# Output projection of two thirds of the sequence rows moved into the spare rows of the recurrence's own output projection

## Chip, cores and metric

One NeuronCore of one Trainium2 chip (trn2). The metric is device time of one execution in microseconds (us); lower is better. The kernel runs 64 recurrent steps and everything around them, forward and backward, in one launch. "Stage" times below come from one traced execution of each kernel.

## The reference, cut to what matters

```python
# x (2048 x 640), mem0 (8 x 640), 32 heads of 128, segments of 32 rows
for s in range(64):
    h = concatenate([mem, xn[32*s:32*s+32]])           # 8 memory rows + 32 x rows
    q, k, v = h @ Wq, h @ Wk, h @ Wv                   # 640 -> 32 x 128
    p = softmax(mask(q @ k.T * scale)); o = p @ v
    o = o @ Wo                                         # 4096 -> 640
    mem = o[:8]                                        # carried to the next step
    outs.append(o[8:])
s = concatenate(outs)
out = x + s * silu(swiglu(xn))                         # g below
# the kernel returns out and the gradients of x, mem0, all weights
```

Only the 8 memory rows are recurrent. The x rows of a step can be computed at any time after its memory keys and values exist.

## The kernel before: the parts concerned

Rows are handled in 22 *tiles* of three segments (120 rows: 3 x 8 memory rows, 96 x rows), each tile cut into 8 *units* of four heads. In the forward loop a step's memory rows form a serial chain, and units of x attention are put as fill between its parts ("gaps" W0, W1, W2, G1 to G6). Three cuts:

```python
# --- one step t of the loop (cut) ---
def stage(): return ch.tile([P, 1024], BF16, name="stg", tag="stg", bufs=2)
sk = stage(); half(Wk_, 0, sk, 'v'); half(Wk_, 1, sk, 'v')
gap("W0")
sq = stage(); half(Wq, 0, sq, 'v')
...
dump(sk, k.KS[t])                     # k of the memory rows to memory, SyncE
half(Wq, 1, sq, 'v')
gap("W1")
sv = stage()                          # third tile of two buffers: waits for dump(sk)
...
k.copy(sv[:, 0:512], bA[:], eng='s')  # ScalarE
...
gap("W2")
#   memory scores -> psT
nc.scalar.copy(sTm[:], psT...)        # ScalarE
gap("G1")
#   softmax -> Pm; gap("G2"); transposes -> PTm; gap("G3")
for h in range(H):                    # memory PV: 32 matmuls, 8 columns each
    nc.tensor.matmul(pom[:, h, :], vt[:, h*P:(h+1)*P], PTm[:, h//16, :, h%16], ...)
oTm = ch.tile([P, H, 8], BF16, ...)   # 8 rows; the array's column group has 32
nc.vector.tensor_copy(oTm[:], pom[:])
packed_out(k, pm, oTm, Wo, True, True)   # O projection of the memory rows

# --- a unit of x attention: PV (L656 ff.) ---
for j in range(4):
    nc.tensor.matmul(po[:, j*P:(j+1)*P], PTs[qd%2][0:n, j, :], v[0:n, j*P:(j+1)*P], ...)
nc.scalar.copy(v[0:n], po[0:n])
nc.gpsimd.dma_start(k.OR[...], v[0:n])   # token-major rows, projected later

# --- the gaps of step t (cut) ---
if g == "W0":
    at(pv, t - 1, 0); at(turn_p, t - 1, 2)
    for u in kb[0:2]: ld_k(*u)           # SyncE: k rows of a later tile
elif g == "W1": at(pv, t - 1, 1)
elif g == "W2": at(pv, t - 1, 2)

# --- after the loop: output projection (cut) ---
for g in range(4): nc.sync.dma_start(k.QM[...], k.QVS[...])
nc.gpsimd.dma_start(WoT[:], ...)         # three weights at once, 15.7 MB
for nm_ in ("v", "k"): nc.gpsimd.dma_start(WT[nm_][:], ...)
blocks = [(3*b, 3, 96) for b in range(7)] + [(21, 1, 32)]
work = [(b, qd) for b in range(len(blocks)) for qd in range(8)]   # 64 units
# per unit: load rows of three tiles, 12 transposes, 3 copies, 20 matmuls
# per tile: epilogue out = x + s*g, gradient products, their transposes and stores
nc.gpsimd.dma_start(WT["q"][:], ...)     # fourth weight, then the next phase
```

## Time and profile before

| | before |
|---|---|
| median of the first three runs (range) | 6011.49 us (6007.91 to 6018.85) |
| start up to the first projection matmul of the loop | 614.9 us |
| forward loop, to the last v projection matmul | 1277.4 us |
| tail, to the first load of the output projection | 106.3 us |
| output projection, to the first matmul of the next phase | 264.7 us |
| that product (g0) and the preparation of the backward loop | 162.9 us |
| backward loop, then the rest | 1304.2 and 2276.6 us |

### The profile page before, as it was taken

What the parts mean: (1) busy time and instruction counts of PE and PEld (TensorE: products, weight loads), DVE (VectorE), ACT (ScalarE), POOL (GpSimd) and SP (SyncE); (2) the same over time, 40 slices, a digit from 0 to 9 for tenths busy, and PEclk for the clock granted to TensorE, in tenths of its full rate; (3) what the DMA queues carried; (4) which work ended last, traced back from release to release, by engine and by line L of the source; (5) the groups of instructions that cost most, each with busy time, mean ns of one, the idle gap of its engine ahead of it and who ended that gap; (6) DMA issues with size and microseconds to landing.
All of it is one profiled execution on the core that took longest, in us unless ns stands there. A gap on an engine that the chain in (4) does not pass through costs nothing. (4 is left out here: it accounts for less than half of the span.)

```text
span 6007.0 us, 166595 instructions
## 1 busy us (share of the span) xinstructions
PE 5182.7 (86%) x68354; PEld 3289.8 (55%) x68354; DVE 2394.8 (40%) x7496; ACT 1817.4 (30%) x4945; POOL 1038.9 (17%) x1654
## 2 busy tenths in 40 slices
PE   5969899999996775788888998799999999969899
PEld 2546455555553563555555665555566556637565
DVE  5723455555553333344444453322233223300351
ACT  2424355555553322222223332222232122200110
POOL 0000243434333201233333332000000000000000
PEclk9979899999998886888889998899999999989999
DMA  6565344444446453566556663532243323353332
GB/s 225 163 246 191 97 138 135 138 132 137 134 130 217 124 170 115 147 170 167 162 161 169 175 179 102 131 87 80 77 108 83 85 82 92 100 195 127 106 121 94
DMA packets 928035, 824.48 MB, mean 137 GB/s; under 512 B 403085, under 2 KB 819789, under 8 KB 923285
## 3 DMA queue, kind: packets, MB, share of 16 engines
q1 hardware_dynamic: 755904, 576.97, 32.8%
q0 software_dynamic: 53312, 118.39, 6.9%
q10 hardware_dynamic: 118057, 118.48, 6.2%
q8 instruction: 538, 8.81, 0.6%
q14 instruction: 224, 1.84, 0.1%
HBM read 509.44 MB, written 313.42 MB: 137 GB/s over the span
## 5 line engine op out<-in xcount | busy, mean ns | idle before, releaser
L1331 PE MATMUL wg<-gr,hr 120*128 120x512 bf16 (+1 forms) x2640 | 588.0, 383 | 16.6 <-DVE dST L1263 12.5
L1309 PE MATMUL g<-w,gT 128*128 128x320 bf16 x3840 | 555.6, 302 | 0.0
L1309 PEld LDWEIGHTS <-gT 128*128 128x128 bf16 x3840 | 372.2, 99 | 140.5
L1331 PEld LDWEIGHTS <-hr 120*128 120x128 bf16 (+1 forms) x2640 | 257.6, 99 | 338.9 <-issue 44.8
L1699 POOL TENSOR_TENSOR o<-gxn,ln_G 128x640 bf16<-128x640 f32 x16 | 22.4, 1398 | 2115.2 <-DVE gxn L1697 2115.2
L361 PEld LDWEIGHTS <-gkv 128*8 128x8 bf16 x8192 | 212.8, 98 | 154.6 <-DVE gkv L980 34.0
L90 DVE CAST wgo<-wg 128x512 bf16<-128x512 f32 x72 | 47.5, 688 | 582.8 <-PE wg L1331 295.0
L342 PEld LDWEIGHTS <-hx 128*32 128x32 bf16 x7680 | 178.0, 97 | 165.3 <-issue 5.2
L90 DVE CAST stg<-bank 128x512 bf16<-128x512 f32 x256 | 177.0, 692 | 201.9 <-PE bank L342 200.8
L1276 ACT CAST gr<-r6p 120x512 bf16<-120x512 f32 (+1 forms) x176 | 103.1, 586 | 490.8 <-PE r6p L1273 202.1
L361 PE MATMUL gbank<-WvT,gkv 128*8 128x320 bf16 x4096 | 227.8, 399 | 26.8 <-DVE gkv L980 26.8
L632 ACT ACTIVATE xP<-xsp,xnm 120x120 bf16<-120x120 f32 (+1 forms) x704 | 240.5, 376 | 10.4 <-DVE xnm L628 6.3
L1318 DVE TENSOR_TENSOR ghacc<-ghacc,g 128x320 f32<-128x320 f32 x240 | 117.0, 487 | 289.6 <-PE g L1309 289.6
L1419 PE MATMUL oa<-gow,orr 128*128 128x320 bf16 x1280 | 176.1, 301 | 54.3 <-DMA gow<-GWO 54.3
L92 ACT CAST wgo<-wg 128x512 bf16<-128x512 f32 x48 | 25.8, 589 | 634.9 <-PE wg L1331 634.9
L643 POOL TENSOR_TENSOR xP<-xP,xrz 120x480 bf16<-120x480 bf16 (+1 forms) x176 | 170.4, 968 | 158.9 <-ACT xP L632 107.8
L662 ACT CAST xv<-xpo 120x512 bf16<-120x512 f32 (+1 forms) x176 | 103.3, 588 | 298.8 <-PE xpo L660 247.8
L1115 DVE SCALAR_TENSOR_TENSOR gdS<-gdp,Dx,gPr 120x120 bf16<-120x120 f32 (+1 forms) x704 | 188.7, 330 | 0.0
L92 ACT COPY gT<-t6g 128x960 bf16<-128x960 bf16 (+5 forms) x216 | 167.3, 794 | 57.3 <-PE t6g L1292 55.3
L1419 PEld LDWEIGHTS <-orr 128*128 128x128 bf16 x1280 | 126.0, 98 | 104.5 <-issue 54.7
L1112 DVE CUSTOM_DVE_ANT_0 gdS<-gdp,gPr 120x120 bf16<-120x120 f32 (+1 forms) x704 | 153.5, 273 | 60.6 <-PE gdp L1101 59.9
L1087 POOL DMA_DIRECT2D VTD<-gvT x176 | 129.8, 739 | 272.5 <-ACT gvT L1086 247.1
(312 smaller groups left out, 10952.2 us busy)
## 6 DMA issues: line engine op xcount, KB each, us to landing
QVS<-stg SPq DMA_DIRECT2D x128, 256.0 KB
gqv<-QVS SPq DMA_DIRECT2D x112, 192.0 KB
vTt<-VTD SPq DMA_DIRECT2D x64, 320.0 KB
orr<-OR SPq DMA_DIRECT2D x16, 1280.0 KB
OR<-xv POOLq DMA_DIRECT2D x168, 120.0 KB, 2.9
VTD<-gvT POOLq DMA_DIRECT2D x168, 120.0 KB, 4.6
PR<-xP POOLq DMA_DIRECT2D x168, 112.5 KB, 5.0
gPr<-PR SPq DMA_DIRECT2D x168, 112.5 KB
```

Of the source, the lines that this page charges most:

```text
L90: return nc.vector.tensor_copy(out, in_)
L92: return nc.scalar.copy(out, in_)
L342: k.nc.tensor.matmul(bank[32 * g:32 * g + 32, :], x[:, dc, :], W[:, dc, c0:c0 + 512], start=(dc == 0), stop=(dc == k.DC - 1), tile_positio ...
L361: k.nc.tensor.matmul(pm[p0:p0 + nq, 0:320], x[:, h, :], W[:, h, 320 * b:320 * b + 320], start=(first and i == 0), stop=(last and i == 15), ...
L632: nc.scalar.activation(Pb[0:n, j, 0:n], sp[0:n, j, :], ACT.Exp, bias=nmx[0:n, j:j + 1], scale=k.scale, accum_out=Z[0:n, j:j + 1])
L643: nc.gpsimd.tensor_tensor(Pb[0:n, :, 0:n], Pb[0:n, :, 0:n], bc_last(rz[0:n], n), ALU.mult)
L1087: nc.gpsimd.dma_start(k.VTD[tl][:, :, h0:h0 + 4, :], vTq[:])
L1112: nc.vector.tensor_tensor_reduce(dS[0:n, j, :], dp[0:n, j, :], Pr[0:n, j, :], 1.0, 0.0, ALU.mult, ALU.add, Dx[0:n, j:j + 1])
L1115: nc.vector.scalar_tensor_tensor(dS[0:n, j, :], dp[0:n, j, :], Dx[0:n, j:j + 1], Pr[0:n, j, :], op0=ALU.subtract, op1=ALU.mult)
L1309: nc.tensor.matmul(pg[:], ring[:, i, j, r0:r0 + P], Ws[qd][i][:, j, 320 * h:320 * h + 320], start=(i == 0 and j == 0), stop=(i == 2 and j ...
L1331: nc.tensor.matmul(accs[dc][:], hr[0:n, tl, dc * P:(dc + 1) * P], st["g", NTL * qd + tl, i][0:n, :], start=(tl == 0), stop=(tl == NTL - 1))
L1419: nc.tensor.matmul(ac[j][i][:], orr[:, w, jj * P:(jj + 1) * P], gow[:, w, 320 * i:320 * i + 320], start=(w == 0), stop=(w == NW - 1))
```

## The change

The memory rows' O projection uses 8 of the 32 rows (weight columns) of each column group, and the time of its matmuls hangs on the 320 columns streamed, hardly on those (the 64 matmuls of a step span 2.35 us at the median). So 24 x rows of an older step are to ride along for nothing. For tiles 0 to 13 the PV of a unit is also made transposed, stored, and read back as 24 columns of the weights; their projected rows leave the loop finished, and the output projection after it has 32 units instead of 64. To make room, `vt` is folded over two row groups (half the bytes per partition), so the memory PV runs on two row groups. The output projection is rewritten: one epilogue a unit, in a fixed order, inputs loaded one tile ahead, its stores issued by SyncE, weight fetches cut into 13 pieces.

```diff
-        vt = st.tile([40, HD], BF16, name="vt")
+        vt = st.tile([104, HD // 2], BF16, name="vt")
+        oTm = st.tile([P, H, 32], BF16, name="oTm")
@@ memory PV
-            PTm = ch.tile([40, 2, 8, 16], BF16, name="PTm", tag="PTm")
-            nc.scalar.copy(PTm[:].rearrange("p a q h -> p a (q h)"), ps3[:])
+            PTm = ch.tile([104, 8, 16], BF16, name="PTm", tag="PTm")
+            for a in range(2):
+                nc.scalar.copy(PTm[64 * a:64 * a + 40].rearrange("p q h -> p (q h)"), ps3[64 * a:64 * a + 40])
-            for h in range(H):
-                nc.tensor.matmul(pom[:, h, :], vt[:, h * P:(h + 1) * P], PTm[:, h // 16, :, h % 16], start=True, stop=True)
-            nc.vector.tensor_copy(oTm[:], pom[:])
+            for j in range(16):
+                for a in range(2):
+                    p0 = 64 * a
+                    nc.tensor.matmul(poms[a][:, j, :], vt[p0:p0 + 40, j * P:(j + 1) * P], PTm[p0:p0 + 40, :, j],
+                                     start=True, stop=True, tile_position=(p0, 0))
+            nc.vector.tensor_copy(oTm[:, 0:16, 0:8], poms[0])
+            nc.vector.tensor_copy(oTm[:, 16:32, 0:8], poms[1])
@@ the ride
+        def oride_ld(t):
+                nc.sync.dma_start(r[:], k.OTX[t - k.OT0])               # in gap W0
+        def oride(t):
+                nc.gpsimd.tensor_copy(oTm[:, :, 8:32], uu.pop(("o", t))[:])   # in gap G1
@@ pv
+            if 4 * tl < k.NO:
+                for j in range(4):
+                    nc.tensor.matmul(pt[:, j, :], v[0:n, j * P:(j + 1) * P], PTs[qd % 2][0:n, j, 24:120], start=True, stop=True)
+                nc.scalar.copy(ot[:].rearrange("p c h t -> p h c t"), pt[:].rearrange("p h (c t) -> p h c t", t=24))
+                nc.scalar.dma_start(k.OTX[4 * tl:4 * tl + 4, :, 4 * qd:4 * qd + 4, :]..., ot[:]...)
@@ output projection (cut)
-        blocks = [(3 * b, 3, 96) for b in range(7)] + [(21, 1, 32)]
+        blocks = [(tl, 3, 96) for tl in range(NRT, k.NTL - 3, 3)] + [(k.NTL - 2, 1, 96), (k.NTL - 1, 1, 32)]
+            if tl < NRT:
+                s_tok = io.tile([96, D], BF16, name="s_tok", tag="s_tok", bufs=2)
+                for b in range(2):
+                    nc.scalar.dma_start(s_tok[:, 320 * b:320 * b + 320], k.FS[t0:t0 + 4, 32 * b + 8:32 * b + 32, :])
+            for _ in range(2):
+                if i >= 2 and fetch:
+                    nc.gpsimd.dma_start(*fetch.pop(0))
+            for (f, o) in ((ep_ld, -1), (ep_b, 0), (ep_c, 1), (ep_d, 2)):
+                if i - o in slot:
+                    f(slot[i - o])
```

## The prediction

> **What bounds the kernel now.** I read the page first: one core, span 6007.0 us, TensorE 86% busy. An average over stages says little, so I took the table of windows to cut the span, then inside the stages that the diff touches the groups of instructions, the waits and the timeline, engine by engine. The columns of the table are the window, its length, then busy us (and count) of TensorE, weight loads, VectorE, ScalarE and GpSimd, the granted clock, the DMA share and GB/s.
>
> ```profile
> 1000.00:1300.00 300.00, 284.51 (x5187) 165.23 (x5183) 170.66 (x503) 157.52 (x545) 124.23 (x179) 0.99 0.45 134
> ...
> 1900.00:1960.00 60.00, 9.69 (x77) 6.52 (x77) 4.81 (x16) 9.41 (x39) 13.96 (x16) 0.50 0.88 317
> 1960.00:1999.00 39.00, 18.83 (x222) 13.18 (x222) 9.98 (x42) 21.85 (x102) 20.34 (x33) 0.50 0.29 67
> 1999.00:2030.00 31.00, 24.46 (x228) 19.06 (x229) 5.73 (x16) 3.83 (x8) 0.55 (x1) 0.83 0.42 119
> ...
> 2060.00:2230.00 170.00, 143.36 (x1609) 117.17 (x1608) 66.45 (x172) 42.48 (x87) 14.88 (x17) 0.97 0.51 154
> 2230.00:2263.00 33.00, 4.54 (x88) 3.60 (x87) 4.64 (x13) 2.96 (x7) 4.33 (x4) 0.50 0.63 206
> ```
>
> Four pieces matter. The **forward loop** runs from 614.5 us (first projection matmul) to about 1900: 64 steps of some 20 us, TensorE 95% busy. The **tail**, the last tile's softmax and PV after the last step, goes to 1999; its first 60 us are DMA at 317 GB/s with TensorE idle: the 15.7 MB of transposed weights for the next phase (three of 128x5x4096 elements of 2 bytes) are fetched at once there, and the tail's small loads stand behind them:
>
> ```profile
> 1908.74 16.03 SPq L591 DMA_DIRECT2D xv<-QVS  x1
> ```
>
> The **output projection** goes from the first load of attention rows at 1998.6 to the first matmul of the next phase at 2263.3, 265 us, for 64 work units; its last 22 us are again idle behind a weight fetch:
>
> ```profile
> 1998.57 1.34 SPq L772 DMA_DIRECT2D orow<-OR  x3
> ...
> 2263.29 5.28 PE L891 MATMUL g0pb<-WoT,g0x 128*128 128x512 bf16 x12 [22.04 <-DMA g0x<-GST]
> ```
>
> What comes after (backward loop, weight gradients) the diff leaves alone. In the loop, the memory rows of a step make a serial chain (projections, scores, softmax, PV, output projection, next step), with x-row work as filler. TensorE waits there little; the fillers on ScalarE are nearly as long as the chain. From the groups of 1000 to 1600 us (30 steps; busy, mean ns, then idle before and its releaser):
>
> ```profile
> L660 PE MATMUL xpo<-xv,xPT 120*128 120x128 bf16 x316 | 31.4, 222 | 0.0
> L662 ACT CAST xv<-xpo 120x512 bf16<-120x512 f32 x79 | 46.5, 589 | 132.3 <-PE xpo L660 96.2 <-DMA OR<-xv 23.7 <-DMA KS<-stg 9.7
> L585 ACT COPY kT<-kpt 128x384 bf16<-128x384 bf16 x79 | 34.7, 478 | 4.1 <-PE kpt L583 4.1
> L545 ACT COPY PTm<-bank 40x256 bf16<-40x256 bf16 x30 | 11.0, 366 | 6.8 <-PE bank L543 6.8
> L551 DVE CAST oTm<-bank 128x256 bf16<-128x256 f32 x30 | 12.7, 424 | 11.5 <-PE bank L549 11.5
> ```
>
> **What the Trainium skill says.** (1) "TensorE: Matmul & The Clock Gate", Part 1, "Wait — 56ns, not 53.3ns?": starts of matmuls never come closer than about 25 ns, however small. The trace agrees: the 32 memory-PV matmuls of 8 columns take 1.00 us, less a latency of 0.17 over 31 gaps, 27 ns each. So placing them on two row groups of the array, as the change does, wins nothing. (2) "TensorEngine Tiling (Array Packing)", Key Properties: changing the tiling mode drains the array; the change adds two such changes a step. No row before prices one. (3) "DMA: Bandwidth & Descriptors", "Queues, rings and completion order": each DMA engine takes turns between queue rows at packet granularity. The trace agrees with sharing and no priority: the small load above took 16.03 us to issue beside the weight fetch. (4) "SBUF — State Buffer", the summary of rules: GpSimd and a two-port VectorE copy exclude each other. The new GpSimd copy of 128x768 lands near the eight small VectorE copies of the v rows (291 ns each); what that costs, the trace before cannot say.
>
> **Part by part: the loop.** For tiles 0 to 13 of 22 (steps 4 to 45, 42 steps) each of the 112 PV units gets four more matmuls of 96 columns. Four of 128 columns span 0.40 us less 0.22 of latency, so about 60 ns apart; four of 96 cost about 0.17 us of TensorE. ScalarE gets a copy of 384 columns (0.48 us, the kT row) and the issue of a store (0.44 us, the ACT issue of a load in the later stage). Three units come in two steps of three, two in the third.
>
> In a step of three units the third sits just before the memory scores' copy sTm, in ScalarE's written order. In the timeline, PV ends at 1244.44 us, two stg copies fill ScalarE until 1245.2, then xv, then
>
> ```profile
> 1245.57 0.37 ACT L520 CAST sTm<-bank 40x256 bf16<-40x256 f32 x1
> ```
>
> After the change TensorE comes 0.3 to 0.5 us later (2 to 3 times 0.17), and 0.9 us of new ScalarE work stands ahead of sTm, so sTm comes about 1.3 us later. Not all of it reaches the end: VectorE is busy with v copies until about 1247.05 anyway, and TensorE idles 0.68 us before the transposes of Pm. I carry 0.65 us. In a step of two units no PV stands there: 0.35 us. Then in every step: PTm in two copies of 128 columns instead of one of 256 (from the 256 and 512 rows, 366 and 589 ns, about 0.26 each; the pair of stg copies shows 0.11 us of overlap, so 0.04 more), oTm in two copies (424 against 691 ns for 512 columns gives 0.29 each, so 0.16 more). Sum: 0.85 and 0.55, mean 0.75 us. For drains, the locked port, later loads (each OTX store is 512 pieces of 192 bytes; SyncE issues twice as many v loads) I add 0.25: 1.0 us times 42 = 42 us. The other 22 steps carry 0.2 plus 0.15: 8 us. The output projection of the step keeps its cost: 64 matmuls of 320 columns, four at a time, 16 times 133 ns = 2.1 us against 2.35 seen; 32 columns of weights for 8 change only weight loads that lie under it. **Loop: +50 us.**
>
> **The tail.** The weights come in 13 pieces issued between the tail's own GpSimd instructions, not in three lumps. The instruction order shows, though, that the first piece still goes before the last step's probabilities are stored. The bytes are the same: 15.7 MB at 317 GB/s are 50 us, and the tail from 1901 to 1999 has some 50 to 60 us of work of its own (1949 to 1999 is undisturbed, and does most of it). They overlap better, yet not fully. **Tail: -12 us**, a choice between 0 and -40.
>
> **The output projection.** Work units fall from 64 to 32: two blocks of three tiles (16 units), 8 units of one tile, 8 of 32 rows. A full unit took (2230 - 1999)/57, about 4.0 us, with TensorE at 20 matmuls of 120 ns plus 12 transposes, about 3.0. If the epilogue were free, 40 units of 4 us would be saved, 160 us. It is not: 22 epilogues that were three per eight units come now one per unit. Each costs ScalarE six load issues (0.44 each, 2.6 us) and copies of 0.56 and 0.48, about 3.7 us; VectorE four of 0.49 and two oT copies, 2.7 us; and 0.49 MB of inputs, 0.12 of s rows and 0.37 of stores beside 0.29 of attention rows, 1.27 MB, which at 300 GB/s is 4.2 us. So ScalarE, DMA and TensorE all stand near 4; in one order with few buffers I take 4.6 us for the 16 full units (74), 4.2 for the four after (17), 1 for the other 12 (12), 9 for start and cold clock (0.55 in the first 30 us before), and 24 for the end behind the last weight fetch, which is unchanged (22 before). Sum 136 against 265: **-129 us**.
>
> **Sum.** 6011 - 129 - 12 + 50 = 5920 us, 1.5% less.
>
> **Rivals.** (A) *The loop gives it back.* If ScalarE's store issues also wait for earlier DMAs[...], sTm's whole 1.3 us and more arrive on the chain: 2 us times 42 plus 10 is +94, total about 5965. For it: ScalarE already waits on the KS store (15.5 us in those 30 steps) and its softmax ends at 1253.63, just when the output projection does (1253.46). Against: ScalarE is only 52% busy. (B) *The epilogue becomes the bound.* Loads waiting for the previous tile's loads at 6 us a tile give 20 times 6 in place of 91: 5950. For it: before, ScalarE's gzT copy stood 3.96 us behind load and store issues. (C) *All hidden*: the tail loses its 40 us of stall, extra matmuls slip under waits (0.5 us a step): 5865. Against: TensorE has 5% idle in the loop.
>
> **Range and chances.** The terms err by about 30 (loop), 20 (projection), 15 (tail); in quadrature near 40, so 8 in 10 is about 55 us to either side: 5865 to 5975. Faster by over 2% means below 5891, 29 us under my number: 0.24. Slower by 2% needs a loop cost of over 300 us: 0.02. Within 2%: 0.74.
>
> **What would show it.** In the changed profile: loop period up by about 1 us between steps 8 and 45 and by 0.3 after; a wait of the transposes of sTm on ScalarE that was nearly absent; memory PV still 27 ns a matmul; the projection stage about 136 us, ScalarE issuing loads most of the time; the tail 90 to 100 us. I am wrong if the loop's period rises by over 2 us (A), a tile's epilogue takes over 6 us (B), or the tail falls to 70 us (C).

## More of the kernel before

The stages are cut at instructions that every version has: the first and last matmul that makes the loop's bank from a weight and the step's rows, the first load of attention rows, the first matmul of g0, and so on. A change in one stage can then be read from that stage, while the 86% of TensorE over the whole span tells nothing on it. Two lines of the loop's waits are needed below, from the table of waits over 600 to 1960 us (engine, line, what it waited for: us in total, times, longest):

```profile
ACT stg L92 <- DMA KS<-stg: 28.2, 15, 3.3
PE bank L526 <- ACT sTm L520: 4.0, 7, 1.1
```

In the first line ScalarE's copy of v into its stage tile waits until the dump of k has landed, since three stage tiles share two buffers. 28 us in a loop of 1277 look harmless. In the second, TensorE waits for ScalarE's copy of the memory scores.

## The result, and the profile after

| | before, same chip | after |
|---|---|---|
| median (range) of 4 runs, all fast | 6015.09 us (6007.91 to 6018.85) | 5968.41 us (5955.75 to 5980.50) |
| ratio, 95% interval | | 0.9924 [0.9899, 0.9948] |

The kernel is 0.8% faster. Ratios here are the mean of one kernel's fast runs over the mean of the other's in the same rounds, so not quite the ratio of the medians. The prediction, 5920 us, was 48 us too low; its range held.

| stage, us (one trace each) | before | after | measured change | predicted |
|---|---|---|---|---|
| forward loop | 1277.4 | 1335.5 | +58.1 | +50 |
| tail | 106.3 | 110.5 | +4.2 | -12 |
| output projection | 264.7 | 150.6 | -114.1 | -129 |
| sum of the three | | | -51.8 | -91 |
| start | 614.9 | 619.3 | +4.4 | none |
| everything after | 3743.7 | 3762.6 | +18.9 | none |

The traces differ by 28.5 us, the medians by 46.7: the traced run of before (6008.71 us, taken beside the four) was near the fastest, that of after the slowest. The 18.9 us lie in code that the change leaves alone. Other traces of kernels that share this code have 2276.6 to 2299.7 us in the last part alone, and the kernel before with nothing but two loads of its loop moved (below) has 3763.1 us in everything after. So I take the 18.9 us for the spread of single traces, the 4.4 us of the start too (613.7 to 622.2 in the runs below without initialising stores), and explain only the three stages. They have a spread as well: the same loop took 1335.5 and 1330.3 us in two traces, the same output projection 149.9 to 157.6 in seven.

First the windows of the changed kernel (columns as in the prediction): a piece of the loop, the tail in two pieces, most of the full units of the output projection, the last full and the short ones, and its end.

```profile
1000.00:1300.00 300.00, 269.44 (x4993) 165.94 (x5019) 165.27 (x489) 165.60 (x566) 121.00 (x167) 0.98 0.53 150
...
1955.00:2000.00 45.00, 15.51 (x196) 10.51 (x193) 11.02 (x37) 15.65 (x63) 19.81 (x26) 0.60 0.79 258
2000.00:2030.00 30.00, 7.81 (x90) 5.44 (x91) 4.47 (x16) 9.19 (x47) 10.22 (x15) 0.50 0.65 203
...
2066.00:2140.00 74.00, 48.78 (x487) 38.52 (x488) 32.73 (x79) 12.57 (x27) 0.00 (x0) 0.90 0.84 231
2140.00:2193.00 53.00, 34.17 (x559) 30.43 (x555) 24.60 (x65) 12.80 (x25) 0.31 (x1) 0.81 0.60 164
2193.00:2216.00 23.00, 0.42 (x7) 0.42 (x8) 1.84 (x4) 0.97 (x2) 1.43 (x1) 0.57 0.77 256
```

The stretch of full units has TensorE busy 66% (48.78 of 74) where before it was 84%, and the DMA engines 84% where before they were at 51%. The tail's small loads still stand behind the weight fetch (timeline of SyncE), and at the end TensorE is still idle for 18.6 us in one piece beside a fetch (timeline of TensorE):

```profile
1965.10 10.19 SPq L611 DMA_DIRECT2D xq<-QVS  x1
```

```profile
2215.91 4.47 PE L965 MATMUL g0pb<-WoT,g0x 128*128 128x512 bf16 x10 [18.61 <-DMA gqv<-QVS]
```

In the loop, groups of 1000 to 1600 us (28 steps), answering to those of the prediction:

```profile
L693 ACT CAST xoT<-xot 128x384 bf16<-128x384 f32 x72 | 34.6, 481 | 95.3 <-PE xot L691 94.9 <-DMA OTX<-xoT 0.4
...
L691 PE MATMUL xot<-xPT,xv 120*128 120x96 bf16 x288 | 24.8, 209 | 0.0
L682 POOL COPY oTm<-oride 128x768 bf16<-128x768 bf16 x28 | 23.3, 831 | 0.0
...
L562 ACT COPY PTm<-bank 40x128 bf16<-40x128 bf16 x56 | 14.5, 259 | 8.3 <-PE bank L559 8.0
...
L570 DVE CAST oTm<-bank 128x128 bf16<-128x128 f32 x28 | 8.2, 292 | 8.6 <-PE bank L568 5.5 <-ACT xP L652 0.2
...
L542 PE MATMUL bank<-ident,sTm 40*128 40x40 bf16 x58 | 6.3, 184 | 15.6 <-ACT sTm L536 15.6
```

The durations are those predicted (0.48 us for the added ScalarE copy, 0.26 and 0.29 for the halved copies), and the predicted wait for sTm is there: 15.6 us in 28 steps, which the same group of the kernel before had at 1.6 in 30. What the prediction did not have is the growth of another line, in the same table of waits as above:

```profile
ACT stg L92 <- DMA KS<-stg: 37.4, 21, 5.7
...
PE bank L542 <- ACT sTm L536: 23.9, 36, 2.6
```

And memory PV on two row groups (timeline of TensorE, one step of before, one of after; start, us):

```profile
1106.15 1.00 PE L549 MATMUL bank<-PTm,vt 40*128 40x8 bf16 x32
```

```profile
1108.24 0.67 PE L568 MATMUL bank<-PTm,vt 40*128 40x8 bf16 x32 [0.30 <-ACT PTm L562]
```

The same 32 matmuls take a third less, where the prediction saw nothing to win.

### The profile page after: what moved, and what is told of

It reads as the page before. It is cut to its first block, busy times and chain, and to the rows that moved or that the text cites. A ratio compares the mean times of both kernels' runs of the same rounds, so it can differ in the third digit from the quotient of the medians.

```text
span 5978.5 us, 165521 instructions
## 1 busy us (share of the span) xinstructions
PE 5060.8 (85%) x67367; PEld 3238.0 (54%) x67644; DVE 2395.6 (40%) x7482; ACT 1840.4 (31%) x5059; POOL 1045.7 (17%) x1647
## 5 line engine op out<-in xcount | busy, mean ns | idle before, releaser
L1405 PEld LDWEIGHTS <-hr 120*128 120x128 bf16 (+1 forms) x2640 | 258.7, 99 | 343.2 <-issue 51.8
L663 POOL TENSOR_TENSOR xP<-xP,xrz 120x480 bf16<-120x480 bf16 (+1 forms) x176 | 170.0, 966 | 162.8 <-ACT xP L652 95.6
L529 DVE COPY vt<-stg 8x512 bf16<-8x512 bf16 x512 | 162.8, 318 | 51.4 <-ACT stg L92 44.0
```

Of the source, the lines that this page charges most:

```text
L529: nc.vector.tensor_copy(vt[p0:p0 + 8, c0:c0 + 512], sv[32 * g:32 * g + 8, b * 512:(b + 1) * 512])
L663: nc.gpsimd.tensor_tensor(Pb[0:n, :, 0:n], Pb[0:n, :, 0:n], bc_last(rz[0:n], n), ALU.mult)
L1405: nc.tensor.matmul(accs[dc][:], hr[0:n, tl, dc * P:(dc + 1) * P], st["g", NTL * qd + tl, i][0:n, :], start=(tl == 0), stop=(tl == NTL - 1))
```

## The experiments

Each run is timed beside the kernel before on its chip: four executions of each experiment, and seven of the kernel before for the batch. Ratios are to the kernel before; the changed kernel has 0.9924.

### First batch: take parts of the change away

**The added PV away, zeros ride** (the rows that ride are zeros). Its output is wrong, which doesn't matter for the time.

```diff
+        for i in range(k.NO):                      # before the loop
+            nc.gpsimd.dma_start(k.OTX[i]..., kTs[0]...)
-            if 4 * tl < k.NO:                      # xot matmuls, copy, store: gone
-                ...
```

> The changed kernel without the extra PV work (no 96-column matmuls, no ScalarE copy, no store to OTX; OTX is filled once with zeros, so the result is wrong on purpose). The step's output projection still carries 32 rows, the GpSimd copy and its load stay. Loop = first Wk matmul to last Wv matmul: 1277.4 us before, 1335.5 after. Theory (the extra PV units are the loop's cost, 0.9 us in each of 42 steps, as the shortest periods of the two traces say): loop about 1295, the last 20 us being later transfers and the wider step. Rival (the ride itself, its GpSimd copy, load and 32 rows, is the cost): loop over 1320.

Measured: 5996.55 us (5986.24 to 6011.45), ratio 0.9956; the start is 23 us longer by the 56 initialising stores, so only the loop counts. It fell by 11 us only, to 1324.6. A tile goes by in three steps, so there are three kinds of step: the first and the second with three PV units, the third with two. Periods (from one step's write of the next step's rows to the next) of the early steps did fall by what the PV should cost (steps 4 to 20, lower quartiles of the three kinds: 20.95, 20.29, 20.24 to 20.15, 19.33, 19.59), but in steps 21 to 45 those of the first kind grew (21.29 to 22.83). The time came back in one wait:

```profile
ACT stg L92 <- DMA KS<-stg: 56.2, 25, 5.6
```

This points to a step that is not the sum of its engines' work: in some steps with most fill, the landing of the dump of k would be a second bound (tested in the second batch). The sequence shows in the changed kernel's SyncE timeline of one such step:

```profile
1332.58 0.34 SPq L677 DMA_DIRECT2D oride<-OTX  x1
1332.97 1.34 SPq L275 DMA_DIRECT2D kr<-KS  x2
1335.40 0.34 SPq L501 DMA_DIRECT2D KS<-stg  x1
```

and in ScalarE's, the copy that needs the dumped buffer:

```profile
1340.97 1.07 ACT L92 CAST stg<-bank 128x512 bf16<-128x512 f32 x2 [1.03 <-DMA KS<-stg]
```

The loads for the ride and for k stand ahead of the dump in one queue, and the copy waits 5.6 us after the dump's issue.

**No ride at all, but the split, the fixed order and the paced fetch kept.**

```diff
-        self.OTX = mk("OTX", (self.NO, P, H, 24))
+        self.NO = 0
-        blocks = [(tl, 3, 96) for tl in range(NRT, k.NTL - 3, 3)] + ...
+        blocks = [(3 * b, 3, 96) for b in range(7)] + [(21, 1, 32)]
```

> Nothing rides: all 22 tiles go through the output projection, 64 units as before, but with the new order of the epilogue, the fetches in pieces, the memory PV on two row groups and the 32-row step. Theory: loop 1277 to 1290; projection about 250 (before 264.7), since an epilogue of a tile costs more than the 4.0 us unit it stands beside; tail about 108 as in both; in all within 20 us of before. Rival (the fixed order is what won the 114 us of the projection): projection under 200 and time under 5950.

Measured: correct, 6039.98 us (6034.39 to 6045.05), ratio 1.0029. Output projection 255.9 us: all of its rewriting but the halved units is worth 9 us, so these carry 105 of the 114. Steps without this wait were shorter than before in the second kind (19.42 against 19.57 us, means of steps 21 to 45), yet the loop was 7 us longer (1284.8), again with a longer wait for the dump (40.4 us from step 21 on, 26.1 before). That left the price of the split open until the last batch.

**The memory PV unsplit, a badly made test.** To fit, both halves of v were put in the same partitions, one over the other.

```diff
-        vt = st.tile([104, HD // 2], BF16, name="vt")
+        vt = st.tile([40, HD // 2], BF16, name="vt")
-                    dst = vt[64 * i + 8 + a:64 * i + 8 + b, :]
+                    dst = vt[8 + a:8 + b, :]
```

> The changed kernel with the memory PV back on one row group: one transposed PTm of 256 columns in one copy, 32 matmuls in a row, one VectorE copy of oTm. For want of room the v rows of heads 16 to 31 lie over those of heads 0 to 15, wrong on purpose; loads and copies are as many. The prediction (the split wins nothing and costs 0.2 us a step): loop 13 us shorter than 1335.5. The trace of the changed kernel (32 matmuls in 0.67 us, not 1.00, and steps that carry no extra PV 0.16 us shorter than before): loop 5 to 12 us longer.

Measured: 6169.59 us (6167.17 to 6184.79), ratio 1.0247, loop 1517.1 us. Its time tells nothing of row groups: the second load of a step had to wait for the first, and SyncE stood still (its waits):

```profile
SPq L473 <- DMA vt<-QVS: 270.0, 86, 5.5
```

The values were wrong by this as well, though within the tolerance of the comparison. The loop's 182 us more come with this stall; as the run also let PTm share a buffer with sTm, they are not split up. One thing it does show: with the changed kernel around them, the 32 matmuls on one row group take 1.00 us again (median of 64 steps; 0.67 on two), so the 0.33 us are the split's.

**The written order kept from the loop through the output projection**, so that the fetch cannot slip into the tail.

```diff
-        start = len(nc.cur_bb.bb.instructions)
+        start = k.start3 = len(nc.cur_bb.bb.instructions)
-        in_order(k, start)            # of the output projection
+        in_order(k, k.start3)
```

> The changed kernel, but each engine has to keep the written order from the loop to the end of the output projection, so that no weight fetch is issued before the tail's own GpSimd work is through. Theory (the tail is long because its small loads share the DMA engines with the fetches): tail from 110.5 to about 65 us; the same bytes then fall on the projection, which grows from 150.6 to 180 or 200; in all 10 us faster to 10 us slower. Rival (the tail is a chain of its own and the fetch lies beside it): tail over 95.

Measured: correct, 5995.60 us (5981.90 to 6014.96), ratio 0.9955. The tail fell from 110.5 to 62.0 us, the output projection rose from 150.6 to 209.8: together 271.8 against 261.1. The windows of both stages:

```profile
1955.00:2017.00 62.00, 40.43 (x543) 26.15 (x544) 24.24 (x84) 35.52 (x150) 31.16 (x46) 0.66 0.37 99
2017.00:2227.00 210.00, 94.90 (x1062) 75.31 (x1062) 60.46 (x154) 29.61 (x72) 25.99 (x39) 0.70 0.80 241
```

The tail has 62 us of work of its own and moves 5.1 MB for it. In the changed kernel it takes 48.5 us more and moves 24.9 MB: besides the 15.7 MB of weights, a copy of 4.2 MB (QM) falls there, as in the kernel before. 19.8 MB in 48.5 us are 408 GB/s. At 317 GB/s, the mean of the kernel before over 60 us, they would take 63 us; at 431, its fullest slice of 2.7 us, 46 (both estimates). So little of the fetch is hidden behind the tail's own work, at most some 14 us.

### Second batch: one wait at a time

**The third unit's PV after the memory scores.**

```diff
-                at(pv, t - 1, 2)      # gap W2
                 ride_ld(t + 1)
             elif g == "G1":
                 oride(t)
+                at(pv, t - 1, 2)
```

> Only the place of the third unit's PV (with its added xot matmuls) in a step changes: after the copy of the memory scores instead of ahead of it. Theory L1 (a step is as long as the sum of its engines' work on the path, as predicted): the wait for the ScalarE copy of the memory scores (18.5 us in 21 steps after the change, 2.6 us before) goes, the loop falls from 1335.5 by 10 to 18 us, the time by as much. Theory L2 (in the three-unit steps the landing of the dump of k is a second bound): that wait goes too, but the wait of ScalarE's stage copy for the dump grows from 31.6 us by most of the gain, and the loop falls by at most 6 us.

Measured: correct, 5973.68 us (5969.59 to 5982.30), ratio 0.9916. The loop stayed (1339.6). In the window 1045 to 1930 us the wait for sTm fell from 18.5 to 5.3 us, and the wait for the dump did not grow but fell (31.6 to 24.7). So neither theory had the mechanism; other steps lengthened (second kind, steps 21 to 45, mean 20.50 to 21.75), and I did not find by what.

**The loads one gap later, behind the dump of k.**

```diff
             if g == "W0":
-                oride_ld(t)
                 at(pv, t - 1, 0)
                 at(turn_p, t - 1, 2)
-                for u in kb[0:2]:
-                    ld_k(*u)
             elif g == "W1":
+                oride_ld(t)
+                for u in kb[0:2]:
+                    ld_k(*u)
                 at(pv, t - 1, 1)
```

> The loads of the ridden tile and of two k tiles are issued one gap later, so that the dump of k goes to its queue ahead of them; nothing else changes. L2: the wait of the stage copy for that dump (31.6 us in 20 steps) falls under 10 us, and the loop falls by 15 to 25 us to 1310 to 1320, the time by as much. L1 or 'the dump is late for another reason' (bandwidth, not order): the wait stays over 22 us and the loop stays within 6 us of 1335.

Measured: correct, 5947.02 us (5940.32 to 5953.61), ratio 0.9870 [0.9853, 0.9887]. The loop fell by 27.1 us to 1308.4, more than the 15 to 25 expected. SyncE's timeline has the dump first:

```profile
1325.24 0.34 SPq L501 DMA_DIRECT2D KS<-stg  x1
1325.69 0.37 SPq L677 DMA_DIRECT2D oride<-OTX  x1
1326.10 1.68 SPq L275 DMA_DIRECT2D kr<-KS  x2
```

and in the table of waits over 600 to 1960 us the wait is all but gone:

```profile
ACT stg L92 <- DMA KS<-stg: 2.1, 4, 1.3
```

Shown, then, as the bytes stayed: the place of the loads ahead of the dump made the wait, and it cost the changed kernel about 27 us of loop in these traces (by the two timed ratios 0.5%, some 30 us).

**Epilogue inputs two tiles ahead, three buffers.**

```diff
-                t_ = io.tile([96, D], BF16, name=f"ep_{nm_}", tag=f"ep_{nm_}", bufs=2)
+                t_ = io.tile([96, D], BF16, name=f"ep_{nm_}", tag=f"ep_{nm_}", bufs=3)
-            for (f, o) in ((ep_ld, -1), (ep_b, 0), (ep_c, 1), (ep_d, 2)):
+            for (f, o) in ((ep_ld, -2), (ep_b, 0), (ep_c, 1), (ep_d, 2)):
```

> The epilogue's loads in the output projection are issued two tiles ahead instead of one, with a third buffer. Theory P1 (latency: VectorE stands for the tile of results that the loop left in memory, and the copies of the next unit stand behind it in its written order): a full unit falls from 5.2 to 4.4 us, the stage from 150.6 to about 138, the time by 10 to 14. Theory P2 (bandwidth: a full unit moves 0.30 MB of rows and about 1.05 MB for one epilogue tile, at the 231 GB/s of that stretch 5.8 us): the stage stays within 4 us of 150 and VectorE only waits elsewhere.

Measured: correct, 5973.92 us (5958.98 to 5979.99), ratio 0.9918: no difference from the changed kernel's. The sixteen full units fell from 85.1 to 79.2 us, the stage only by 3.1 to 147.5. Other traces agree: 85.1, 86.7 and 89.4 us where the loads come one tile ahead, 79.2 and 81.8 where two. But most of it only moved: the start of the stage, to the first matmul of a unit, grew from 6.4 to 11.0 us (10.6 in the trace with 81.8). Latency is a small part of a unit, 0.4 us of 5.3 at most, and net of the start about 0.1.

**The fetch later and in paces** (strict order; 5.2 MB over the loop's drain, the rest beside the second half of the output projection and beside g0).

```diff
+            if t - T < DC:                         # drain of the loop
+                nc.gpsimd.dma_start(k.WoT[:, t - T], src[:, t - T])
+            if i >= 16 and i % 2 == 0 and fetch and i < 31:
+                nc.gpsimd.tensor_copy(dm[:], st["t", ...][0:1, 0, 0:8])   # paces the next line
+                nc.gpsimd.dma_start(*fetch.pop(0))
```

> The written order holds from the loop through the output projection, and the weights for the backward loop are fetched later and in paces: one of them over the drain of the loop, one and the query copy in the second half of the output projection, two beside the product that follows. Theory F1 (the tail's 110 us and the 22 us ahead of the next product are fetched bytes that compete with the path): tail 60 to 70, output projection 125 to 150, next product and its sequel (162 us together) up to 15 longer; time 55 to 85 below the changed kernel, 5885 to 5915. Theory F2 (the same bytes only move on, as they did with the strict order alone): tail 62, but the sum of tail, projection, product and sequel stays within 20 us of the changed kernel's 423.

Measured: correct, 5977.56 us (5952.03 to 5990.75), ratio 0.9916. Tail 80.8, output projection 166.9, g0 and preparation 169.0: 416.7 against the changed kernel's 423.0 from the end of the loop to the backward loop. F2 holds in the sum: the bytes move on (its tail of 62 did not come, as the first weight lay there). The tail is again nearly a plain sum: 62 for itself and 18.8 for 5.2 MB (16.5 at 317 GB/s).

### Third batch: with the dump ahead of the loads

**The same reordering in the kernel before** (the edit above without `oride_ld`).

> The kernel before, with the k loads one gap later and nothing of the change. The kernel before lost 26.1 us in 13 steps to the wait for the dump of k, so L2 expects its loop to fall from 1277 to 1250 to 1260 and the time by 15 to 25 us. With the loop of the changed kernel so ordered (1308.4) that leaves 50 to 58 us for the change in the loop, as predicted (50). If instead the loop stays at 1270 or more, the wait was made large by the change and the ride costs under 40 us without it.

Measured: correct, 6005.14 us (6002.23 to 6015.99), ratio 0.9969. The loop fell by 13.9 us to 1263.5; the expected 17 to 27 was too much, since of 23.6 us of wait that went, about 10 had not shown in the loop:

```profile
ACT stg L92 <- DMA KS<-stg: 4.6, 4, 1.5
```

So with this wait out of both kernels the change costs the loop 1308.4 - 1263.5 = 44.9 us. Of the 58.1 measured, the other 13.2 are the second bound, which bit harder once the ride put more in front of it. A difference of four single traces with some 5 us of spread each would be weak alone, but the timed runs say the same: with the loads moved in both kernels their ratios stand at 0.9870 to 0.9969, which is 0.9901 where it was 0.9924, 14 us.

**No added PV, loads moved** (wrong).

> Wrong on purpose: the changed kernel without the added PV (rows of zeros ride instead), now with the k loads one gap later. Without the late dump taking the time back, L2 expects the removal to shorten the loop by 0.65 to 0.97 us in each of 42 steps, 27 to 41 us below 1308.4, to 1267 to 1281; with the loads as they were it had taken off only 11. If the loop falls by under 15 us, something else than the dump gave the time back.

Measured: 5940.24 us (5939.24 to 5942.08), ratio 0.9863. The loop fell from 1308.4 to 1276.5 us, by 31.9: the removal that had brought 11 us now brings its price, 0.76 us in each of 42 steps. L2 is confirmed by this run and by the move of the loads (its sizes for the later PV and for the kernel before missed).

**Both moves**, and **both moves with early epilogue loads**.

> The changed kernel with both moves: k loads one gap later, third unit's PV after the memory scores. The dump's wait being gone, the removal of the wait for the score copy (5.8 us in 16 steps are left of it with the k loads moved) should now show in full: loop 1300 to 1305, time 3 to 8 us below the k loads alone. If the loop is 1308 or more, the copy's wait is hidden anyway and the place of that PV is worth nothing.

> Both moves and the epilogue's loads two tiles ahead: the candidate for a version that beats both kernels. Loop as in the run with both moves, output projection 3 us shorter; time 5940 plus or minus 10, ratio to the kernel before 0.984 to 0.988.

Measured, both correct: 5946.75 us (5934.71 to 5948.84), ratio 0.9869, loop 1305.8; and 5937.64 us (5931.04 to 5945.90), ratio 0.9859 [0.9842, 0.9876], loop 1302.0, sixteen full units 81.8. The later PV is worth some 3 to 6 us of loop at most, which the times do not separate. The last is a version that beats both kernels: 1.4% under the kernel before, 0.65% under the changed one by the two ratios.

### Fourth batch and after: the two terms still open

**Fewer packets at the same bytes** (transposed gradients laid out in another way; 128 pieces of 960 bytes in place of 640 of 192), on the last version. Its output is wrong, which doesn't matter for the time.

```diff
-            nc.sync.dma_start(k.GZT[:, 96 * tl:96 * tl + nx].rearrange("(dc p) t -> p dc t", p=P), gzT[:, :, 0:nx])
+            dst = k.GZT.rearrange("d s -> (d s)")[...].rearrange("(p a b) -> p a b", p=P, a=DC)
+            nc.sync.dma_start(dst.rearrange("p a b -> p (a b)"), gzT[:].rearrange("p a b -> p (a b)"))
```

> Wrong on purpose in what reads the transposed gradient later: as the run with both moves and early epilogue loads, but each tile of it goes to a contiguous stretch, as 128 pieces of 960 bytes instead of 640 pieces of 192; the bytes stay. In the changed kernel's 70 us of full units 9096 of 22380 packets were under 512 bytes. Theory S (DMA time per packet bounds a full unit): the sixteen full units fall from 81.8 us to 74 or less, the DMA share of that stretch falls from 0.85, and the GB/s rise from 229 or the share falls to under 0.75. Theory V (VectorE's and TensorE's written order bounds it): the sixteen units stay within 3 us of 82 while the share falls.

Measured: 5939.92 us (5931.42 to 5941.94), ratio 0.9862; the sixteen units 81.4 us. In 78 us of full units the packets under 512 bytes fell from 10665 to 1948 and the DMA share from 0.84 to 0.79, and no time came of it. Packet count as the bound is excluded.

**The split alone, loads moved** (no ride).

> The memory PV on two row groups, its two softmax and result copies and the written order stay, the ride goes; the k loads are one gap later. Loops with the k loads so placed: the kernel before 1263.5, zeros riding without the added PV 1276.5, the changed kernel 1308.4. The prediction gave the split 0.2 us in each of 64 steps, 13 us: loop 1276. The reading of clean steps (19.57 before, 19.42 with the split) says it saves 0.15 in some and costs nothing in the rest: loop 1255 to 1264, so that the 13 us between 1263.5 and 1276.5 belong to the ride's load, copy and wider weights.

Measured: correct, 6011.06 us (5996.61 to 6018.53), ratio 0.9982. Loop 1258.6 against 1263.5 unsplit: the split, all its parts together, costs nothing and may save a few us (traces of like kernels with the moves span 1300.9 to 1305.8, so 5 us is near the spread). The prediction had given it +13.

**The ridden rows' loads issued by SyncE instead of ScalarE**, on the same version.

```diff
-                    nc.scalar.dma_start(s_tok[:, 320 * b:320 * b + 320], k.FS[...])
+                    nc.sync.dma_start(s_tok[:, 320 * b:320 * b + 320], k.FS[...])
```

> As the run with both moves and early epilogue loads, but the two loads a tile of the results that the loop left are issued by SyncE instead of ScalarE. In a full unit of that run ScalarE spends 2075.19 to 2080.43, 5.24 us, in its written order: six load issues to 2078.87, then its two copies. Theory Q (ScalarE's order with its load issues is the bound of a full unit): 1.3 to 1.5 us of issue leave it, the sixteen units fall from 81.8 to 60 to 70 us, the time by 12 to 20 to about 5922. Theory V (another engine's order, VectorE and TensorE handing on to each other, or DMA): the sixteen units stay within 4 us of 82.

Measured: correct, 5943.39 us (5935.05 to 5951.72), ratio 0.9854; sixteen units 80.0 us. Theory Q falls. ScalarE's four other issues simply spread out, about 1 us apart.

**A quarter fewer bytes at the same instructions** (epilogue inputs loaded in half their columns). Its output is wrong, which doesn't matter for the time.

```diff
-                t_ = io.tile([96, D], BF16, name=f"ep_{nm_}", tag=f"ep_{nm_}", bufs=3)
-                nc.scalar.dma_start(t_[0:nx, :], src[x0:x0 + nx, :])
+                t_ = keep[nm_][tl % 3]
+                nc.scalar.dma_start(t_[0:nx, 0:D // 2], src[x0:x0 + nx, 0:D // 2])
```

> Wrong on purpose: as the run with both moves and early epilogue loads, but each of the four epilogue inputs is loaded only in its first 320 of 640 columns, into kept tiles (the other half is zero). Instructions, issues and engine work stay; a full unit's bytes fall by 4 times 61 KB, 0.25 of about 1.14 MB, 22%. Theory D (the DMA engines, busy 0.84 to 0.86 of the time at 227 to 236 GB/s in every version, bound a full unit): the unit falls from 5.1 to about 4.0 us (to 4.2 at best if the next bound is near), the sixteen from 81.8 to 64 to 70. Theory V (waits between engines in their written order): the sixteen stay within 4 us of 82 and the DMA share falls to about 0.67.

Measured: 5923.29 us (5921.91 to 5927.24), ratio 0.9856 to a faster-running kernel before (6010.90); sixteen units 73.1 us, 0.54 us less for each, the stage 141.8 against 151.5; the timed ratio (0.9859 for the same version with whole loads) does not resolve this gain. The window of full units:

```profile
2040.00:2100.00 60.00, 49.26 (x468) 37.64 (x467) 33.63 (x80) 12.31 (x27) 0.00 (x0) 0.89 0.73 201
```

It falls between the two theories. Bytes are part of the bound (8.7 of 81.8 us for 22% of the bytes; pure bandwidth would have given 18), and waits between engines are the rest. Each single suspect is worth at most half a microsecond a unit; how the rest is shared among the engines' order stays open.

## Where the prediction was right and where it was wrong, point by point

- **Bounds and stages: right.** The stage cuts held, and the change acted in the three stages named and nowhere else.
- **The loop, +50 against +58.1: nearly the right sum from wrong parts.** Its working adds up engine work. With the dump's wait removed from both kernels that sum is 44.9, and its parts are: split -4.9 (predicted +13), carrying the ride without its PV +17.9 (predicted about 14, as reserve and leftovers), the added PV +31.9, 0.76 us a step (predicted 0.35 to 0.65, mean 0.55, so 23). That these errors cancel to 5 us is luck. The missing 13.2 us are a second bound which the sum has no place for. The prediction had seen that wait ("ScalarE already waits on the KS store") and filed it under rival A; A's size (+94) was wrong, its first piece of evidence was the wait that bit.
- **Within the carrying: the collision that point (4) of the prediction left open is there.** While GpSimd copies the ridden columns (0.83 us), a VectorE copy of v rows can stand still. It happened to 19 of the 56 GpSimd copies: the VectorE copy then ended 0.14 to 0.16 us after the GpSimd one and had taken up to 1.38 us, and the 512 v copies grew from 147.9 to 162.8 us together. In the four kernels without a ride none took over 0.42 us. Before and after (durations in ns, shortest, median, longest):

```profile
L513 DVE COPY vt<-stg x512: 273/282/414, 622.7 to 1894.2; 8x512 bf16<-8x512 bf16 x171
```

```profile
L529 DVE COPY vt<-stg x512: 273/284/1380, 627.8 to 1956.7; 8x512 bf16<-8x512 bf16 x171
```

How much of the 15 us reaches the loop is not separated: with both moves 43 of the 56 collide, and the loop is no longer for it.
- **The failed claim inside the loop's sum:** that two row groups win nothing because starts never come closer than 25 ns. The runs show 0.67 us for 32 matmuls in place of 1.00 (and 1.00 again in the unsplit run); with the same 0.17 of latency that is 16 ns a start. The same page of the Trainium skill, "TensorE: Matmul & The Clock Gate", Part 3, "The mechanism" and "Measured speedup vs the span model", says that matmuls on different row groups run concurrently with starts about 4 ns apart. Pairs 4 ns apart and 27 ns from pair to pair would average 15.1, (16 x 4 + 15 x 27) / 31, an estimate from that page and the trace before; 16 agrees. In the trace the gaps alternate, often 10 and 17 ns: about 27 from one start to the next on the same row group, as before. The floor was read as holding for the array when it holds within a row group.
- **The tail, -12 against +4.2: the step that failed** is "they overlap better, yet not fully". Cutting the fetch into pieces gave no more overlap than the three lumps had: 62 us of own work and 48.5 beside it make 110.5, against 106.3 before. The strict order and the later fetch both moved the bytes, and the time moved with them, at about the bandwidth's price. The prediction's 15.7 MB also left out the 4.2 MB of QM, which lie in the tail of both kernels.
- **The output projection, -129 against -114.1: the mechanism was right, two terms were mis-sized.** Read from TensorE's timeline of the changed kernel:

| term | predicted | measured |
|---|---|---|
| start | 9 | 6.4 |
| 16 full units | 74 (4.6 each) | 85.1 (5.3 each) |
| 4 units of one tile with an epilogue | 17 | 16.1 |
| 12 other units | 12 | 19.5 |
| end behind the weight fetch | 24 | 23.5 |
| sum | 136 | 150.6 |

The full unit: the estimate took 1.27 MB at 300 GB/s for 4.2 us; the stretch moved 231 GB/s with the DMA engines busy 84%. Load latency (0.4 us) and bytes (0.54 us for 22% of them) both count (the latency mostly comes back in the start); packets and ScalarE's issues do not. The other units: four of one tile took 1.8 us each, and the eight of 32 rows, 0.9 us each when nothing is in the way, lose time to waits for rows and to the epilogue of the last but one tile (12.1 us together). The prediction's remark on the start, a clock of 0.55 in the first 30 us, is a misreading: its own line for 1999 to 2030 has 0.83.
- **Signs.** Seen as announced: the wait for sTm, and a mean period up by 1.16 us in steps 8 to 45. Not as announced: 0.77 us from step 46 on (0.3), 16 ns a matmul of memory PV (27), a tail of 110.5 us (90 to 100), an output projection of 150.6 (136).
- **Rivals.** B (6 us a tile) came nearest in this stage with 5.3. C did not occur. Of the 48 us by which the total missed, the three terms make 39 in these traces (8 loop, 16 tail, 15 output projection): all erred the same way, while the range took their errors as independent.

## What to carry to other kernels

A free slot in a matmul is not free work: here the ride saved 105 us of output projection and cost 45 in the loop (with the split), plus 13 by a wait that was already there. Before adding loads to a queue, look for a store behind them on which a two-buffer tile hangs; moving three loads behind one store gave 27 us, more than half of what the whole change had gained. And when a fetch stands beside a latency-bound stretch, price all its bytes at the bandwidth and give no credit for overlap until a trace shows it.

## What the Trainium skill lacked or had wrong

- "TensorE: Matmul & The Clock Gate", Part 1, "Wait — 56ns, not 53.3ns?": the floor of about 25 ns is stated without its limit to one row group; on two row groups the runs show 16 ns a start on average (0.67 us for 32). Part 3 of the page has the exception, but the two places do not point to each other.
- "TensorEngine Tiling (Array Packing)", Key Properties: the drain at a change of tiling mode has no price. Two such changes a step, as the prediction counts them, were not measured alone; with the shorter PV that they come with they cost nothing visible here (loop 1258.6 us with them, 1263.5 without, 64 steps).
- "DMA: Bandwidth & Descriptors", Specifications: 512 bytes are given as the least transfer for line rate. In this stretch larger pieces bought nothing: 10665 packets under 512 bytes made into 1948 left the units at 81.4 us (81.8), while the DMA share fell from 0.84 to 0.79.
- No page gives a rate for a mixed stream of loads and stores in packets of 0.7 to 1 KB on average; the runs show 227 to 236 GB/s at 0.84 to 0.86 busy (229 at 0.79 with the larger packets), against 317 GB/s at 0.88 in the stretch of the weight fetch.
